# The o products of the attention by single heads, in two row halves of the array and two PSUM banks, and spread between second-layer products

## The chip, the cores and the metric

The kernel runs as one program on one core of a Trainium2 chip. The metric is the device time of one execution in microseconds. Before the change the median of three runs is 1733.42 us (1733.07 to 1734.48).

## What is computed

A linear attention over 8 batches, 8 heads, 576 positions and a head dimension of 64 feeds two mixing blocks of width 512 over the same positions:

```python
kv = np.einsum('bhsd,bhse->bhde', k, v)
out = np.einsum('bhsd,bhde->bhse', q, kv)
rms = np.sqrt(np.mean(out * out, axis=-1, keepdims=True) + 1e-06)
x = out / rms * g_norm                      # then (batch, 576, 512)
mixed = np.real(np.fft.fft(np.fft.fft(x, axis=1), axis=2))
u = x + mixed
ch = np.maximum(layer_norm(u) @ w_ch1, 0.0) @ w_ch2
x = u + ch
h = (x.transpose(0, 2, 1) @ U @ V).transpose(0, 2, 1)
u = x + h
return u + np.maximum(u @ w_ch1b, 0.0) @ w_ch2b
```

The change touches the second line alone, the product of q with the 64 by 64 matrix kv of each head, called the o products here.

## The kernel before

The weights of the first block are split into a high and a low part, and three products of the parts stand for one exact one. The positions of all batches together make nine blocks of 512. For each block a loop runs over `NF` = 16 slices of the hidden layer; step `n` emits on TensorE the first-layer products of slice `n` (`emit_l1`, lines 223 to 225, twelve of 128x512) and then the second-layer products of slice `n - 1` (`emit_l2`, lines 252 to 254, twelve of 128x512). All engines work in the order in which the kernel emits; nothing is reordered by a planner. The attention and the Fourier transform of batch `b` are cut into small tasks that hang on the steps of block `b - 1`: the list `side[n]` is run after the second-layer products of step `n`, and a single entry `fill[n]` is run between the first-layer products of step `n` and the second-layer products that follow them. `batch_tasks(b)` makes the lists `t[0]` to `t[13]` for the 16 steps. Batch 0 is computed before the loop starts, batch 1 beside block 0 (steps 0 to 15, in which weights are still being converted and the second-layer products are those of line 244), and batches 2 to 7 beside blocks 1 to 6.

`t_o(b, k)` makes one tile of the o products: up to 128 positions (98 in tile `k` = 4) by 512 columns. The matrices kv of two heads stand as two diagonal blocks of 64 by 64 in a 128 by 128 block of the buffer `kvbd`, whose other two blocks are zero. One product of TensorE takes 128 rows of q (two heads) as the stationary operand and 128 columns of `kvbd` as the moving one, and four products (line 397) fill the 512 columns of one PSUM bank. ScalarE then squares the bank (line 399), VectorE multiplies it by the norm's weight (line 401), sums the squares by head (line 404), scales (line 405), and GpSimd takes the power -1/2 (line 406). `t_norm` applies that a step later (lines 422 and 424). PSUM banks for such tasks come from `side_bank`: in the loop a ring of two banks (`ps_s`), before the loop six banks. Tiles 0 and 1 of a batch hang on step 0, tiles 2 and 3 on step 1, tile 4 on step 2; each pair runs back to back on TensorE.

Before the loop, `t_o(0, 0)` to `t_o(0, 4)` follow `t_kv_first`, and `keep_warm(54)` (line 413), 54 products of an identity, follows them on TensorE ahead of the first transform products (`seq_dft`, lines 495 to 501).

Of the kernel before, what the change touches and what calls it, by code (L numbers as in the profile page):

```python
# [13 lines left out]
AF = mybir.ActivationFunctionType  # L14
ALU = mybir.AluOpType
# [4 lines left out]
B, H, S, D = 8, 8, 576, 64  # L20
# [3 lines left out]
C = 128  # L24
# [7 lines left out]
NF = DFF // 128  # L32
# [13 lines left out]
def kernel(ctx: ExitStack, tc: tile.TileContext, qT, kvm, gn, w1a, w2a, w1b, w2b,  # L46
                      ucat, v4, tabs, outT):
    nc = tc.nc
# [14 lines left out]
    def whole(pool, shape, dt, name, tag=None, bufs=1):  # L63

        n = int(np.prod(shape[1:]))
        t = pool.tile([shape[0], -(-n // 16) * 16], dt, tag=tag or name, name=name, bufs=bufs)[:, 0:n]
        if len(shape) == 2:
            return t
        names = "abcd"[:len(shape) - 1]
        return t.rearrange(f"p ({' '.join(names)}) -> p {' '.join(names)}", **dict(zip(names, shape[1:])))  # L70
# [3 lines left out]
    def side_bank(nm):  # L74
        if early:
            k = len(early) % 6
            early.append(True)
            if k < 4:
                return ps_acc.tile([128, 512], F32, tag=f"acc{k}", name=nm)
        return ps_s.tile([128, 512], F32, tag="side", name=nm)  # L80
# [186 lines left out]
    gnb = at.tile([C, D], F32, name="gnb")  # L267
# [34 lines left out]
    kvbd = com.tile([128, 4, 128], F32, tag="kvbd", name="kvbd")  # L302
# [7 lines left out]
    def t_kv_mm(b, half):  # L310
        kv = st[b]["kv"]
        ps = kvps[b, half] = side_bank(f"kv{b}_{half}")
        for j in range(2):
            cols = slice(256 * half + 128 * j, 256 * half + 128 * j + 128)
            for t in range(KC):
                nc.tensor.matmul(out=ps[:, 128 * j:128 * j + 128], lhsT=kv[:, 0, t, cols], rhs=kv[:, 1, t, cols],
                                 start=(t == 0), stop=(t == KC - 1))
# [63 lines left out]
    def kv_back(b):  # L381
        for p in range(2):
            x = slice(64 * p, 64 * p + 64)
            nc.sync.dma_start(out=kvbd[x, :, x], in_=kv_d[b][p])
# [3 lines left out]
    def t_o(b, k):  # L388
        s = st[b]
        g, c, m = OT[k]  # L390
        if k == 0:
            s["x"] = at.tile([C, 2, 3, DM], F32, tag="xpn", name=f"x{b}")
            s["sq"] = at.tile([C, 5, DM], F32, tag="slot_b", name=f"sq{b}")
            s["ss"] = whole(at, [C, 5, H], F32, f"ss{b}", "ss", 2)
        ps = side_bank(f"o{b}_{k}")
        for j in range(4):
            nc.tensor.matmul(out=ps[:m, 128 * j:128 * j + 128], lhsT=s["q"][:, j, C * k:C * k + m],  # L397
                             rhs=kvbd[:, j, :], start=True, stop=True)
        nc.scalar.activation(out=s["sq"][:m, k, :], in_=ps[:m, :], func=AF.Square)
        heads = lambda v: v.rearrange("p (h d) -> p h d", d=D)  # L400
        nc.vector.tensor_tensor(out=heads(s["x"][:m, g, c]), in0=heads(ps[:m, :]),
                                in1=gnb[:m].unsqueeze(1).to_broadcast([m, H, D]), op=ALU.mult)
        ss = s["ss"][:m, k]
        nc.vector.reduce_sum(out=ss, in_=s["sq"][:m, k].rearrange("p (h d) -> p h d", d=D), axis=AX.X)
        nc.vector.tensor_scalar(out=ss, in0=ss, scalar1=1.0 / D, scalar2=EPS, op0=ALU.mult, op1=ALU.add)
        nc.gpsimd.tensor_tensor(out=ss, in0=ss, in1=nhalf[:m, :], op=ALU.pow)
# [8 lines left out]
    def t_norm(b, k):  # L415
        s = st[b]
        g, c, m = OT[k]
        xv = s["x"][:m, g, c].rearrange("p (h d) -> p h d", d=D)
        rs = s["ss"][:m, k]
        if b == 1 or b == 0 and k in (1, 2):  # L420
            for h in range(8):
                nc.scalar.activation(out=xv[:, h], in_=xv[:, h], func=AF.Copy, scale=rs[:, h:h + 1])
        else:
            nc.vector.tensor_tensor(out=xv, in0=xv, in1=rs.unsqueeze(2).to_broadcast([m, H, D]), op=ALU.mult)
        if c == 2:
            nc.scalar.activation(out=s["x"][0:RL + 1, 1, 2], in_=s["x"][64:64 + RL + 1, 0, 2], func=AF.Copy)

    def t_fold_s(b, c, p):
        s = st[b]
        if c == 0 and p == 0:  # L430
            s["f"] = at.tile([C, 2, 3, DM + 256], F32, tag="slot_a", name=f"f{b}")
            s["eh"] = at.tile([C, 2, 2, 2, 256], F32R, tag="slot_b", name=f"eh{b}")
            s["ez"] = at.tile([97, 2, 256], F32R, tag="ez", name=f"ez{b}")
            s["e288"] = e288[32:33]
        m = C if c < 2 else RL
        f, x = s["f"], s["x"]
        eng = nc.gpsimd if b and p else nc.vector
        eng.tensor_tensor(out=f[:m, p, c, 0:DM], in0=x[:m, 0, c], in1=x[:m, 1, c], op=(ALU.add, ALU.subtract)[p])

    def t_fold_e(b, c, p):  # L440
        m = C if c < 2 else RL
        f = st[b]["f"][:m, p, c]
        nc.vector.tensor_tensor(out=f[:, DM:DM + 256], in0=f[:, 1:257], in1=f[:, 511:255:-1],
                                op=(ALU.add, ALU.subtract)[p])
# [10 lines left out]
    def t_fold_h(b, c, p):  # L455
        s = st[b]
        f = s["f"][:, p, c]
        if c < 2:
            nc.scalar.activation(out=s["eh"][:, p, 0, c], in_=f[:, DM:DM + 256], func=AF.Copy)
        else:  # L460
            if p == 0:
                nc.scalar.activation(out=s["e288"], in_=f[32:33, DM:DM + 256], func=AF.Copy)
            pile(s["ez"][:, p], f[:, DM:DM + 256])
        if p == 0:
            m = C if c < 2 else RL
            nc.scalar.activation(out=xe0[:m, c, b:b + 1], in_=f[:m, 0:1], func=AF.Copy)

    def t_fold_l(b, c, p):
        s = st[b]
        f, eh = s["f"][:, p, c, DM:DM + 256], s["eh"]  # L470
        if c < 2:
            nc.vector.tensor_tensor(out=eh[:, p, 1, c], in0=f, in1=f32(eh[:, p, 0, c]), op=ALU.subtract)
        else:
            if p == 0:
                nc.vector.tensor_tensor(out=s["e288"], in0=f[32:33], in1=f32(s["e288"]), op=ALU.subtract)
            pile_low(s["ez"][:, p], f)
# [28 lines left out]
    def t_s1(b, p, ec):  # L505
        t_s1_mm(b, p, ec)
        t_s1_out(b, p, ec)
# [72 lines left out]
    def load_kv(b):  # L580
        kv = at.tile([128, 2, KC, DM], F32, tag="slot_a", name=f"kv{b}")
        for a in range(2):
            nc.sync.dma_start(out=kv[:, a], in_=kvm[b][:, a])
        st.setdefault(b, {})["kv"] = kv

    def batch_tasks(b):

        t = [[] for _ in range(14)]
        d, d1 = 0, SH if b == 1 else 0
        for c in range(3):  # L590
            ks = range(2 * c, min(2 * c + 2, 5))
            t[c + d][0:0] = [lambda k=k: t_o(b, k) for k in ks]
            t[c + d + 1] += [lambda k=k: t_norm(b, k) for k in ks]
            t[c + d + 3] += [lambda c=c, p=p: t_fold_s(b, c, p) for p in range(2)]
            t[c + d + 3].append(lambda c=c: t_fold_e(b, c, 0))
            t[c + d + 4] += [lambda c=c: t_fold_e(b, c, 1)]
            for p in range(2):
                t[c + d + 4 + p].insert(0, lambda c=c, p=p: t_fold_h(b, c, p))
                t[c + d + 4 + p].append(lambda c=c, p=p: t_fold_l(b, c, p))
            if c == 2 and 1 < b < B - 1 and b + 1 not in EARLY:  # L600
                fill[(b - 1) * NF + 11] = lambda: t_s2(b, 2)
            else:
                t[c + 9].append(lambda c=c: t_s2(b, c))
        for p in range(2):
            if d1:
                fill[8 + p] = lambda p=p: [t_s1(b, p, e) for e in range(2)]
            else:
                t[7 + p] += [lambda p=p, e=e: t_s1(b, p, e) for e in range(2)]
        if b + 1 < B:
            if b + 1 in EARLY:  # L610
                t[11].insert(0, lambda: kv_back(b + 1))
            else:
                t[7].append(lambda: load_kv(b + 1))
                for h in range(2):
                    t[11 + h].append(lambda h=h: t_kv_mm(b + 1, h))
                    t[12 + h].insert(0, lambda h=h: t_kv_out(b + 1, h))
            t[12].append(lambda: load_q(b + 1))
        return t
# [632 lines left out]
    fill = {}  # L1251
# [10 lines left out]
    with tc.manual_schedule():  # L1262
# [188 lines left out]
        def heads(n):  # L1451
            if n in mags:
                w_mags(*mags[n])
            if n + 2 < NP:
                split_w1(n + 2)

        for n in range(NP):
            i, j = n % NF, n // NF
# [143 lines left out]
```

## Time and profile before

| | |
|---|---|
| median of 3 runs | 1733.42 us |
| the profiled execution, its own time | 1734.35 us |
| its span, first to last instruction | 1732.6 us |
| granted TensorE clock, mean | 0.999 |

The page names the busy time of each engine: PE is the products on TensorE, PEld its weight loads, DVE is VectorE, ACT is ScalarE, POOL is GpSimd. A product of two 4-byte float operands (`f32` buffers) is executed as two records, one load and one product each: the 40 tiles have 160 products in line 397, and the trace has 320 records of each kind. A record's duration is longer than the step from one record to the next, because they overlap; the steps are read from the starts.

### The profile page before, as it was taken

How to read it: one execution, taken by the hardware profiler on the slowest of the kernel's cores; microseconds unless marked ns; L12 is line 12 of the kernel's file. 1: busy time of each engine (PE TensorE's matmuls, PEld its weight loads, DVE VectorE, ACT ScalarE, POOL GpSimd, SP SyncE). 2: the span in 40 equal slices, each digit the busy share in tenths (PEclk: the TensorE clock that was granted, in tenths of full speed). 3: DMA queues.
4: the chain of work that ended last, by engine and by line, in shares of the span. 5: the costliest groups of instructions: out<-in, count | busy, mean ns of one | idle time of the engine just before them, and what ended most of it. 6: DMA issues, size and time to landing. Idle time of an engine off the chain costs nothing.

```text
span 1732.6 us, 23201 instructions
## 1 busy us (share of the span) xinstructions
PE 1716.3 (99%) x8222; PEld 1426.1 (82%) x8222; DVE 1184.6 (68%) x1903; ACT 830.8 (48%) x1592; POOL 462.3 (27%) x362
## 2 busy tenths in 40 slices
PE   8999999999999999999999999999999999999999
PEld 8767788888888888888888888888888888888887
DVE  5899767778677686756676666448835963694285
ACT  5774344544435343343556565456445534552253
POOL 2346454455645446443322223000000000000000
PEclk9999999999999999999999999999999999999999
DMA  8666024150613416113368864767776776777676
GB/s 335 224 205 214 30 100 142 37 193 19 229 65 122 178 42 225 34 38 101 118 241 313 321 223 165 249 173 254 252 240 192 240 264 199 222 231 244 194 221 192
DMA packets 129011, 315.24 MB, mean 182 GB/s; under 512 B 20712, under 2 KB 20984, under 8 KB 127104
## 3 DMA queue, kind: packets, MB, share of 16 engines
q1 hardware_dynamic: 128896, 313.77, 54.4%
q8 instruction: 65, 1.06, 0.3%
q14 instruction: 50, 0.41, 0.1%
HBM read 238.83 MB, written 74.88 MB: 181 GB/s over the span
## 4 chain that ended last, share of the span: by engine, by line
PE 92%; DVE 0%; ACT 0%; issue 0%
PE y L1159 10%; PE yy L1239 10%; PE h L223 8%; PE h L224 8%; PE h L225 8%; PE acc L252 7%; PE acc L254 7%; PE acc L253 7%; PE z L1239 5%; PE zz L1159 5%; PE w L1239 3%; PE z L1159 3%; PE o L397 2%; PE pt L855 1%; PE u L880 1%; PE acc L257 1%
## 5 line engine op out<-in xcount | busy, mean ns | idle before, releaser
L199 POOL TENSOR_TENSOR w1l<-w,w1h 128x512 fp32r<-128x512 f32 x147 | 197.4, 1343 | 399.7 <-ACT w1h L198 384.2
L223 PE MATMUL h<-xl,w1h 128*128 128x512 f32 x576 | 231.1, 401 | 1.6 <-DVE xl L710 1.6
L225 PE MATMUL h<-xh,w1l 128*128 128x512 f32 x576 | 224.6, 390 | 0.5 <-POOL w1l L199 0.5
L224 PE MATMUL h<-xh,w1h 128*128 128x512 f32 x576 | 224.8, 390 | 0.0
L252 PE MATMUL acc<-w2h,gl 128*128 128x512 f32 x524 | 205.6, 392 | 0.0
L254 PE MATMUL acc<-w2h,gh 128*128 128x512 f32 x524 | 204.1, 390 | 0.0
L253 PE MATMUL acc<-w2l,gh 128*128 128x512 f32 x524 | 204.0, 389 | 0.0
L232 ACT ACTIVATE gh<-h 128x512 fp32r<-128x512 f32 x147 | 87.5, 595 | 227.3 <-PE h L225 224.9
L1159 PE MATMUL y<-xv,v 128*128 128x512 f32 x768 | 187.5, 390 | 2.7 <-ACT g L1096 2.7
L1096 ACT ACTIVATE g<-y 128x512 f32<-128x512 f32 x128 | 76.6, 598 | 204.1 <-PE y L1159 204.1
L1159 PEld LDWEIGHTS y<-xv,v 128*128 128x128 f32 x768 | 143.9, 188 | 34.1 <-ACT g L1096 4.4
L233 DVE SCALAR_TENSOR_TENSOR gl<-h,gh 128x512 fp32r<-128x512 f32 x147 | 100.8, 686 | 87.8 <-ACT gh L232 86.7
L209 DVE TENSOR_TENSOR w2l<-w,w2h 128x512 fp32r<-128x512 f32 x147 | 136.7, 930 | 34.1 <-ACT w2h L208 33.6
L223 PEld LDWEIGHTS h<-xl,w1h 128*128 128x128 f32 x576 | 108.3, 188 | 24.4 <-ACT w1h L198 2.1
L225 PEld LDWEIGHTS h<-xh,w1l 128*128 128x128 f32 x576 | 108.2, 188 | 24.3 <-POOL w1l L199 0.9
L224 PEld LDWEIGHTS h<-xh,w1h 128*128 128x128 f32 x576 | 108.4, 188 | 22.1 <-issue 1.9
L252 PEld LDWEIGHTS acc<-w2h,gl 128*128 128x128 f32 x524 | 98.4, 188 | 21.2 <-DVE gl L233 1.5
L254 PEld LDWEIGHTS acc<-w2h,gh 128*128 128x128 f32 x524 | 98.4, 188 | 20.6
L253 PEld LDWEIGHTS acc<-w2l,gh 128*128 128x128 f32 x524 | 98.4, 188 | 19.6
L208 ACT ACTIVATE w2h<-w 128x512 fp32r<-128x512 f32 x147 | 91.8, 625 | 40.8 <-PE acc L254 37.3
L198 ACT ACTIVATE w1h<-w 128x512 fp32r<-128x512 f32 x160 | 99.9, 624 | 12.3 <-DVE w L130 12.1
L1090 DVE TENSOR_TENSOR g<-zz,g 128x512 f32<-128x512 f32 x64 | 44.2, 691 | 89.7 <-ACT g L1096 77.4
(244 smaller groups left out, 3666.9 us busy)
## 6 DMA issues: line engine op xcount, KB each, us to landing
v<-wv_d SPq DMA_DIRECT2D x224, 512.0 KB, 3.7
wv_d<-vo SPq DMA_DIRECT2D x112, 256.0 KB, 3.0
kve<-in_kvm SPq DMA_DIRECT2D x40, 256.0 KB, 5.6
q<-in_qT SPq DMA_DIRECT2D x8, 1220.0 KB, 10.0
x_d<-res SPq DMA_DIRECT2D x36, 256.0 KB, 2.0
x2f<-x_d SPq DMA_DIRECT2D x36, 256.0 KB, 5.4
outT<-o SPq DMA_DIRECT2D x36, 256.0 KB, 2.7
u_d<-x SPq DMA_DIRECT2D x32, 256.0 KB, 2.1
```

Of the source, the lines that this page charges most:

```text
L198: nc.scalar.activation(out=ah, in_=a, func=AF.Copy)
L199: (nc.vector if n in on_dve else nc.gpsimd).tensor_tensor(out=al, in0=a, in1=f32(ah), op=ALU.subtract)
L209: nc.vector.tensor_tensor(out=cl, in0=c, in1=f32(ch), op=ALU.subtract)
L223: nc.tensor.matmul(out=h, lhsT=ah[:, kc, :], rhs=xl[:, kc, :], start=(kc == 0), stop=False)
L224: nc.tensor.matmul(out=h, lhsT=ah[:, kc, :], rhs=xh[:, kc, :], start=False, stop=False)
L225: nc.tensor.matmul(out=h, lhsT=al[:, kc, :], rhs=xh[:, kc, :], start=False, stop=(kc == 3))
L233: nc.vector.scalar_tensor_tensor(out=gl, in0=h, scalar=0.0, in1=f32(gh), op0=ALU.max, op1=ALU.subtract)
L252: nc.tensor.matmul(out=a, lhsT=gl[:, tt], rhs=ch, start=s, stop=False)
L253: nc.tensor.matmul(out=a, lhsT=gh[:, tt], rhs=cl, start=False, stop=False)
L254: nc.tensor.matmul(out=a, lhsT=gh[:, tt], rhs=ch, start=False, stop=e)
L1159: nc.tensor.matmul(out=dst, lhsT=w[:, c], rhs=r[:, k], start=p in (0, 1, 3) and k + n == 0, stop=k == 1 and n == 2, skip_group_check=True)
L1239: nc.tensor.matmul(out=dst[mp], lhsT=w[:, c], rhs=r, start=p in (0, 1, 6, 3) and i + n == 0, stop=i == 7 and n == 2, skip_group_check=True)
```

## The change

`t_o` takes two banks for a tile. Each product now takes 64 rows of q and the 64 by 64 block of one head; the even heads use partitions 0 to 63 and write the first 256 columns of one bank, the odd heads use partitions 64 to 127 and write the other bank. So a tile has eight products of 64 rows, 128 stationary columns and 64 moving columns in place of four of 128, 128 and 128. ScalarE and VectorE read each bank for itself, with 256 columns each. For batches 2 to 7 the odd tiles go to `fill`, ahead of the second-layer products of steps 1 and 2, and the even tiles stay in `side`, so that no two tiles follow each other on TensorE without products of a layer between them. Batch 1 and batch 0 keep their order.

```diff
-        ps = side_bank(f"o{b}_{k}")
+        ps = [side_bank(f"o{b}_{k}_{p}") for p in range(2)]
         for j in range(4):
-            nc.tensor.matmul(out=ps[:m, 128 * j:128 * j + 128], lhsT=s["q"][:, j, C * k:C * k + m],
-                             rhs=kvbd[:, j, :], start=True, stop=True)
-        nc.scalar.activation(out=s["sq"][:m, k, :], in_=ps[:m, :], func=AF.Square)
-        heads = lambda v: v.rearrange("p (h d) -> p h d", d=D)
-        nc.vector.tensor_tensor(out=heads(s["x"][:m, g, c]), in0=heads(ps[:m, :]),
-                                in1=gnb[:m].unsqueeze(1).to_broadcast([m, H, D]), op=ALU.mult)
+            for p in range(2):
+                e = slice(64 * p, 64 * p + 64)
+                nc.tensor.matmul(out=ps[p][:m, 64 * j:64 * j + 64], lhsT=s["q"][e, j, C * k:C * k + m],
+                                 rhs=kvbd[e, j, e], start=True, stop=True)
+        heads = lambda v, p: v.rearrange("p (h e d) -> p h e d", e=2, d=D)[:, :, p]
+        for p in range(2):
+            pv = ps[p][:m, 0:256].rearrange("p (h d) -> p h d", d=D)
+            nc.scalar.activation(out=heads(s["sq"][:m, k, :], p), in_=pv, func=AF.Square)
+            nc.vector.tensor_tensor(out=heads(s["x"][:m, g, c], p), in0=pv,
+                                    in1=gnb[:m].unsqueeze(1).to_broadcast([m, H // 2, D]), op=ALU.mult)
...
-            t[c + d][0:0] = [lambda k=k: t_o(b, k) for k in ks]
+            if b == 1:
+                t[c + d][0:0] = [lambda k=k: t_o(b, k) for k in ks]
+            else:
+                for k in ks:
+                    n = (k + 1) // 2
+                    if k % 2:
+                        fill[(b - 1) * NF + n] = lambda k=k: t_o(b, k)
+                    else:
+                        t[n].insert(0, lambda k=k: t_o(b, k))
```

## Rows read from the trace of the kernel before

**Rows 1.** The page: busy time by engine, and the chain that ended last.
```profile
PE 1716.3 (99%) x8222; PEld 1426.1 (82%) x8222; DVE 1184.6 (68%) x1903; ACT 830.8 (48%) x1592; POOL 462.3 (27%) x362
...
PE 92%; DVE 0%; ACT 0%; issue 0%
```

**Rows 2.** TensorE in order of time, batch 7: start, length, operation, count.
```profile
713.75 0.39 PE L254 MATMUL acc<-w2h,gh 128*128 128x512 f32 x1
713.98 1.95 PE L397 MATMUL o<-kvbd,q 128*128 128x128 f32 x16
715.68 0.48 PE L223 MATMUL h<-xl,w1h 128*128 128x512 f32 x1
716.00 0.40 PE L224 MATMUL h<-xh,w1h 128*128 128x512 f32 x1
...
721.23 1.04 PE L397 MATMUL o<-kvbd,q 128*98 128x128 f32 x8
722.02 0.48 PE L223 MATMUL h<-xl,w1h 128*128 128x512 f32 x1
```

**Rows 3.** Weight loads by line and shape: busy us, mean ns, idle before.
```profile
L397 PEld LDWEIGHTS o<-kvbd,q 128*128 128x128 f32 x256 | 32.3, 200 | 4.4 <-DVE kvbd L338 2.1 <-ACT kvr L377 0.9 <-issue 0.5
...
L397 PEld LDWEIGHTS o<-kvbd,q 128*98 128x98 f32 x64 | 7.8, 164 | 1.1 <-issue 0.5
...
L541 PEld LDWEIGHTS s<-tab,y 128*34 128x34 f32 x32 | 3.5, 109 | 0.5
...
L696 PEld LDWEIGHTS ftr<-ident,un 128*128 128x128 f32 x12 | 1.3, 140 | 0.6 <-issue 0.5
...
L696 PEld LDWEIGHTS ftr<-ident,un_z 33*128 33x128 f32 x4 | 0.3, 138 | 0.1
```

**Rows 4.** Weight loads in order of time: two after a pause, four of 33 rows.
```profile
50.01 0.32 PEld L696 LDWEIGHTS ftr<-ident,un_z 33*128 33x128 f32 x4
...
55.56 0.19 PEld L223 LDWEIGHTS h<-xl,w1h 128*128 128x128 f32 x1 [1.78 <-ACT w1h L198]
55.67 0.19 PEld L224 LDWEIGHTS h<-xh,w1h 128*128 128x128 f32 x1
```

**Rows 5.** TensorE in order of time around 34-column products.
```profile
668.88 0.39 PE L225 MATMUL h<-xh,w1l 128*128 128x512 f32 x1
669.11 0.28 PE L541 MATMUL s<-tab,y 128*34 128x258 f32 x1
...
670.53 0.40 PE L252 MATMUL acc<-w2h,gl 128*128 128x512 f32 x1
```

**Rows 6.** ScalarE and VectorE from PSUM, by line and shape, blocks 1 to 6.
```profile
L399 ACT ACTIVATE sq<-o 128x512 f32<-128x512 f32 x24 | 14.3, 595 | 17.7 <-PE o L397 17.6
...
L545 ACT ACTIVATE de<-s 128x258 f32<-128x258 f32 x12 | 4.6, 387 | 35.3 <-PE s L543 35.3
...
L401 DVE TENSOR_TENSOR x<-o,gnb 128x512 f32<-128x512 f32 x24 | 16.4, 685 | 9.9 <-ACT sq L399 9.9
...
L546 DVE TENSOR_TENSOR de<-s,de 128x258 f32<-128x258 f32 x12 | 5.0, 419 | 22.8 <-ACT de L545 22.8
```

**Rows 7.** Batch 1 in order of time, TensorE and ScalarE.
```profile
65.73 2.05 PE L397 MATMUL o<-kvbd,q 128*128 128x128 f32 x16 [0.70 <-ACT kvr L377]
...
75.52 0.48 PE L223 MATMUL h<-xl,w1h 128*128 128x512 f32 x1
...
77.05 1.06 ACT L399 ACTIVATE sq<-o 128x512 f32<-128x512 f32 x2
```

**Rows 8.** Batch 0 in order of time.
```profile
20.39 12.22 PE L413 MATMUL warm<-ident 128*128 128x128 f32 x108
32.37 0.38 PE L495 MATMUL s<-tab,eh 128*128 128x290 f32 x1
```

**Rows 9.** Batch 4, first tile, in order of time: TensorE and VectorE.
```profile
387.39 1.95 PE L397 MATMUL o<-kvbd,q 128*128 128x128 f32 x16
...
390.02 0.68 DVE L401 TENSOR_TENSOR x<-o,gnb 128x512 f32<-128x512 f32 x1
```

## Prediction, made before the changed kernel was run

> **What bounds the kernel now.** First the page's busy times and its chain that ended last: TensorE is busy 99% of the span and 92% of the chain is its products; VectorE (68%), ScalarE (48%) and GpSimd (27%) follow it [rows 1]. So work on those three costs nothing while TensorE's next instruction isn't kept waiting, and a nanosecond on TensorE is a nanosecond of the span. Then TensorE in order of time around one pair of tiles and one single tile [rows 2]: the reader should take starts, not lengths. Between 512-column products a start follows a start in 0.23 us (713.75 to 713.98). The 16 records of two tiles run from 713.98 to 715.68, and the next step, 0.32, is 0.09 longer than the usual 0.23. So a pair costs 1.70 + 0.09 = 1.79, a tile 0.893 us and a record 112 ns; the 98-row tile costs 0.79 + 0.09 = 0.88, 109 ns a record. The 30 tiles of batches 2 to 7 are 6 x (4 x 0.893 + 0.88) = 26.7 us, all 40 about 36: that is all that the change can work on.
>
> **What a record of an o product waits for.** A record is a weight load and a product, and a load runs beside the product before it. Two things could set the 112 ns: the load of 128 columns, or the streaming of 128 moving columns. The loads by shape [rows 3] last 200 ns at 128 columns, 164 at 98 and 109 at 34, about 0.9 ns a column over a constant latency; in order of time a load that starts after a pause at 55.56 is followed by the next at 55.67, so 128 columns occupy the load path some 107 ns [rows 4]. Streaming takes about the same: with 98 stationary columns the load shrinks, yet the record still takes 109. Both are at the limit. Rows don't count: of the transposing loads, the one of 33 rows lasts 138 ns and the one of 128 rows 140 [rows 3], and the four of 33 rows follow each other every (0.32 - 0.14) / 3 = 0.06 us although they stream 33 columns only [rows 4]. That is the row that speaks most against the change: it halves the moving columns (streaming 53 ns) and the rows, but each head keeps a load of 128 columns, and there are twice as many, 16 loads of 107 ns a tile in place of 8. Nothing can be won unless two loads are under way at once; if they are, perfectly, the two halves bring the tile back to 0.89.
>
> **The change part by part.**
>
> TensorE, batches 2 to 7. The trace has no two loads into different rows, so the price of a tile lies between both halves overlapped, 8 x 112 = 0.89, and one load after the other, 16 x 112 = 1.79; for the 98-row tile, whose load is about 82 ns, between 8 x 87 = 0.70 and 16 x 87 = 1.39. I take a value between. A float product is two records, so the order is load and product of the even head twice, then of the odd head twice. In the trace a load never starts ahead of the start of the product before it. If that order holds and loads of different halves may overlap, the odd head's first load starts when the even head's second product is taken up, at 107 + 53 = 160 ns, its second at 267, and the next even head's first at 320: 2 x (107 + 53) + about 10 = 330 ns for the four records of two heads. A tile is 4 x 0.33 = 1.32, 0.43 more than now; the 98-row tile 4 x (2 x (82 + 53) + 10) = 1.12, 0.24 more. A batch: 4 x 0.43 + 0.24 = 1.96; six: **+11.8 us**.
>
> Entering and leaving the half-row form: no row shows it in a running stream. Nearest is the 34-column product [rows 5]: it starts 0.23 after the product before, twelve of them take 1.42 or 0.118 each, and the next follows at once. I take 0.3 us for 40 tiles. The Trainium skill, TensorEngine Tiling (Array Packing), Key Properties, says that changing the tiling mode drains the engine; these rows show no drain for narrow columns, and no row shows row halves.
>
> Eviction. ScalarE takes 595 ns for 512 columns and 387 for 258, VectorE 685 and 419 [rows 6]: two halves cost 0.18 and 0.15 us more a tile, some 7 and 6 us over 40 tiles on engines with idle time, while VectorE may read the first bank as ScalarE reads the second (0.39 + 2 x 0.42 = 1.23 against 0.60 + 0.69 = 1.29). Cover: TensorE. It ends where TensorE wants the bank back.
>
> The alternation is needed for just that, since a tile now takes the whole ring of two banks. Between two tiles lie twelve products of a layer, 12 x 0.227 = 2.72 us. The latest eviction is that of the first tile of a batch: its products end near 387.39 + 0.89 + 0.16 = 388.44, the multiply starts at 390.02 behind the adds of the block before and takes 0.68 [rows 9], so it ends 2.3 us after, 2.4 with the split. The next tile starts at 387.39 + 0.893 + 0.09 + 2.72 = 391.09, so it fits by 0.2; I charge nothing, and 0.3 x 6 = 2 us if it does not fit. Behind a late multiply on VectorE queue the reduction, the scaling, and then the low part of the hidden values that second-layer products need (line 233); the odd tiles reach GpSimd's power earlier relative to `t_norm` than the pair does now. No DMA moves.
>
> Batch 1 keeps pairs, so its second tile waits for the first one's banks: end of the last record (0.27 after its start, less the usual step 0.11) + 0.39 + 0.42 + 0.05 = 1.0 us after the first pair. With 1.32 a tile the first pair ends at 65.73 + 1.32 + 1.0 + 1.32 = 69.4, where it ended at 65.73 + 1.79 = 67.52: +1.85. The second pair starts 1.70 ahead of 75.52 [rows 7], now at 75.67, its first tile ends 76.99; ScalarE squares it at 77.2 at the earliest (it came at 77.05 before, busy with weights), the bank is free at 78.05, and the pair ends at 79.4, not 75.52: +3.85. The fifth tile adds 0.24: **+4.1**. Queued behind this on TensorE are the layers of block 0; later waits of theirs may give some back, which I don't count.
>
> Batch 0. `keep_warm` follows the o products and the first transform product starts at its last step, 32.37 [rows 8]: TensorE has no gap there, so the five tiles' 1.96 us pass on: **+2.0**, with 0.4 as the least (VectorE's extra 0.75, partly in its gaps).
>
> Sum: 11.8 + 0.3 + 4.1 + 2.0 = +18.2. The profiled execution is 1734.35 us (span 1732.6 and 1.75 around it), 0.93 above the median of the runs: 1734.35 + 18.2 - 0.93 = **1751.6 us**.
>
> **The rivals.**
>
> Both halves fully overlapped. For: nothing in the rows forbids a load into other rows to start early. Batches 2 to 7: 0 for the large tiles, 6 x -0.18 for the small; batch 1 still waits for banks (end of second pair 78.8, +3.3, less 0.18); batch 0 +0.4; entering 0.3. Sum +2.8, or +1 if block 0 gives some back: 1733.4 + 2.8 = 1736.2. The Trainium skill, the same section, says that different tiles can run loads and products in parallel; by that sentence this would be the case.
>
> One load at a time: the halves do not run together and the change doesn't do what it says. For: in every row loads follow each other. A batch 4 x 0.893 + 0.52 = 4.1: six are 24.6, batch 1 +6.2 (pairs end at 70.3 and 81.2, then 0.5), batch 0 +4.1, entering 0.3: +35.2, 1768.6.
>
> A drain at each change of form, on top of the forecast: what the overlap hides now would show. Entering, 0.39 - 0.23 = 0.16; leaving, 1.04 - 0.79 = 0.25 [rows 2]; 40 x 0.41 = 16.4: 1768. Against it: [rows 5]. The skill's sentence on the drain is this rival.
>
> The other side, faster: a load of 64 rows occupies half the time, and the halves overlap. Then a tile is 8 x 58 = 0.46, 0.43 less: batches 2 to 7 -12.8, batch 1 +2.4 (the second pair still waits for ScalarE at 77.05), entering 0.3: -10.1, 1723.3. It decides from the point where a record of a half takes under 50 ns. Against it: 33 rows load no faster than 128 [rows 3]. For it: those loads are of another form.
>
> **How the numbers follow.** Forecast 0.30, full overlap 0.22, one load at a time 0.24, drain 0.08, faster 0.16. A measurement of this kernel can tell about 0.2%, 3.5 us, from no change. Faster: 0.16 and 0.01 of full overlap, 0.17. Same: most of full overlap, 0.19. Slower: 0.64. The range goes from the middle of the fast case, 1723, to 1772, over the serial one with its unknowns (the 2 us of banks, 1 to 2 of batch 0); about 0.08 lies below and 0.06 above.
>
> **What would show it.** Steps between starts in line 397's records, in blocks 1 to 6: four in 0.33 us (forecast), 0.22 (overlap), 0.45 (serial), under 0.2 (faster). The distance from the last layer product before a tile to the first after it tells the drain. In batch 1 a wait on VectorE's line 401 in front of tiles 1 and 3; in batches 2 to 7 none: such waits would make the alternation the failed step. Wrong altogether would be a kernel that changes by more than 36 us, since only the o products and banks are touched.

## Result, and the profile after

The changed kernel takes 1752.77 us (median; 1750.88 to 1754.32) and the kernel before, run beside it, 1733.95: a ratio of 1.0105 with a 95% interval of 1.0093 to 1.0117, or 18.8 us more. The forecast was 1751.6 and slower. The sum came out nearly right, but by luck: two of its terms were wrong in opposite directions. The profiled execution of after took 1754.32 us, its span is 1752.4.

The page after, busy time by engine and the chain that ended last, answers to [rows 1]:

```profile
PE 1734.5 (99%) x8542; PEld 1431.6 (82%) x8542; DVE 1192.0 (68%) x1943; ACT 833.3 (48%) x1632; POOL 464.5 (27%) x362
...
PE 97%; DMA 1%; DVE 1%; ACT 1%; SPq 0%; issue 0%; POOL 0%; DVEq 0%; ACTq 0%
```

TensorE is the bound as it was. It has 18.2 us more busy time and 320 records more; every other engine gained under 8 us.

TensorE in order of time around one tile of after (start, length, operation, count), to be held against [rows 2]:

```profile
294.81 0.39 PE L225 MATMUL h<-xh,w1l 128*128 128x512 f32 x1
295.13 1.11 PE L399 MATMUL o<-kvbd,q 64*128 64x64 f32 x16
296.17 0.50 PE L223 MATMUL h<-xl,w1h 128*128 128x512 f32 x1
296.51 0.39 PE L224 MATMUL h<-xh,w1h 128*128 128x512 f32 x1
```

The weight loads of the same tile, in three windows: the first 70 ns, the first 170 ns, and the whole.

```profile
295.13 0.19 PEld L399 LDWEIGHTS o<-kvbd,q 64*128 64x128 f32 x2 [0.35 <-issue]
...
295.13 0.30 PEld L399 LDWEIGHTS o<-kvbd,q 64*128 64x128 f32 x4 [0.35 <-issue]
...
295.13 0.97 PEld L399 LDWEIGHTS o<-kvbd,q 64*128 64x128 f32 x16 [0.35 <-issue]
296.17 0.19 PEld L223 LDWEIGHTS h<-xl,w1h 128*128 128x128 f32 x1
```

Two things are to be seen here. First, the halves run together. The first load lasts 0.183 us, and two of them fit into 0.190: they start 7 ns apart. (A record doesn't name its half; that two such loads are of different halves follows from the halves in turn, below, where loads of one half go 0.11 apart.) The next two end 0.11 later. So each pair of loads takes the 0.11 us that one full load took, and 16 records of half the rows cost what 8 full ones did: (0.97 - 0.19) / 7 = 0.11 us a pair. Four records take 0.22, not the 0.33 of the forecast. Second, the way in and out is no longer free. From the layer product to the first record it is 295.13 - 294.81 = 0.32 where it was 0.23, the first load of the tile starts with its product and not beside the one before it, and at the end the load of line 223 starts 0.07 after the last o load has ended, where loads of layer products run ahead.

The cost of a tile follows from four starts: from the layer product ahead of it to the second one behind it, less the two steps of 0.227 that these would take alone. After: 296.51 - 294.81 - 0.454 = 1.25 us. Before: (716.00 - 713.75 - 0.454) / 2 = 0.90 from [rows 2]. So a tile costs 0.35 more, and all 24 large tiles of batches 2 to 7 show it within 0.01; the 98-row tile costs 0.15 more.

Loads and evictions by line and shape (busy us, mean ns | idle before), which answer to [rows 3] and [rows 6]:

```profile
L399 PEld LDWEIGHTS o<-kvbd,q 64*128 64x128 f32 x512 | 35.7, 207 | 14.8 <-issue 6.3 <-DVE ss L408 2.1 <-DVE x L428 2.1
...
L404 ACT ACTIVATE sq<-o 128x256 f32<-128x256 f32 x64 | 21.3, 384 | 30.1 <-PE o L399 30.0
...
L405 DVE TENSOR_TENSOR x<-o,gnb 128x256 f32<-128x256 f32 x64 | 24.1, 416 | 22.2 <-ACT sq L404 22.2
```

The load of 64 rows isn't shorter than the one of 128 rows (0.20 us in [rows 3]). The half evictions took 384 and 416 ns, as estimated.

The start of the kernel shows a third thing that the prediction hadn't looked at, the granted clock. Here are two stretches of each kernel (busy us and instructions of the engines, then the granted clock, DMA share, GB/s). Before:

```profile
15.20:25.40 10.20, 10.20 (x79) 10.20 (x78) 8.34 (x17) 8.06 (x22) 7.51 (x5) 0.83 1.03 408
...
69.80:76.60 6.80, 6.80 (x33) 4.59 (x32) 6.17 (x13) 4.82 (x10) 2.83 (x3) 1.00 0.32 95
```

After:

```profile
15.20:25.40 10.20, 10.20 (x85) 10.08 (x84) 8.33 (x22) 7.47 (x23) 7.28 (x5) 0.50 1.03 409
...
69.80:76.60 6.80, 6.28 (x34) 5.45 (x33) 4.00 (x11) 3.72 (x9) 3.48 (x3) 0.50 0.38 139
```

In after TensorE has half its clock (1.2 of 2.4 GHz) over the o products of batch 0 and the warming products behind them, 10.2 us long, where before had it for a third of that (3.4 us). It has half its clock once more in batch 1, for 6.8 us, where before had the full clock. The length of the first stretch isn't fixed: with the same products in batch 0, the profiled execution of the halves in turn has 10.2 us and that of the pairs kept 6.8 (both below); of the seven with batch 0 as before, six have 3.4 and one has none.

### The profile page after: what moved, and what is told of

The parts are those of the page before. It is cut to its first block, busy times and chain, and to the rows that moved or that the text cites. A ratio compares the mean times of both kernels' runs of the same rounds, so it can differ in the third digit from the quotient of the medians.

```text
span 1752.4 us, 23925 instructions
## 1 busy us (share of the span) xinstructions
PE 1734.5 (99%) x8542; PEld 1431.6 (82%) x8542; DVE 1192.0 (68%) x1943; ACT 833.3 (48%) x1632; POOL 464.5 (27%) x362
## 4 chain that ended last, share of the span: by engine, by line
PE 97%; DMA 1%; DVE 1%; ACT 1%; SPq 0%; issue 0%; POOL 0%; DVEq 0%; ACTq 0%
PE y L1171 10%; PE yy L1251 10%; PE h L223 8%; PE h L224 8%; PE h L225 8%; PE acc L252 7%; PE acc L254 7%; PE acc L253 7%; PE z L1251 5%; PE zz L1171 5%; PE acc L244 3%; PE o L399 3%; PE w L1251 2%; PE z L1171 2%; PE pt L867 1%; PE u L892 1%
## 5 line engine op out<-in xcount | busy, mean ns | idle before, releaser
L198 ACT ACTIVATE w1h<-w 128x512 fp32r<-128x512 f32 x160 | 99.8, 624 | 11.9 <-DVE w L130 11.8
```

The costliest lines, as they stand in the source:

```text
L198: nc.scalar.activation(out=ah, in_=a, func=AF.Copy)
```

## Experiments

**Full rows, 64 columns.** As after, but each product takes all 128 rows of q, so that no two can share the array.

```diff
-                nc.tensor.matmul(out=ps[p][:m, 64 * j:64 * j + 64], lhsT=s["q"][e, j, C * k:C * k + m],
-                                 rhs=kvbd[e, j, e], start=True, stop=True)
+                nc.tensor.matmul(out=ps[p][:m, 64 * j:64 * j + 64], lhsT=s["q"][:, j, C * k:C * k + m],
+                                 rhs=kvbd[:, j, e], start=True, stop=True)
```

> As the changed kernel (two banks, alternation, eight products of 64 moving columns a tile), but each product uses all 128 rows of q, so no form of the array changes and no two loads go to different rows. Theory (the load of 128 columns sets the step, and the changed kernel won back the doubled number of loads only by running the halves side by side): a record every 112 ns, 16 records 1.79 us a tile against the changed kernel's 1.24 from product to product, so +0.55 a large tile and +0.35 to +0.7 a small one, 15 to 17 us over batches 2 to 7; batch 0 and 1 add some 2 to 5: 1768 to 1774 us. If in batch 0 the clock still stays at half for 10 us, half rows are not what held it down; with 3.4 us it would be them. Rival (64 moving columns stream in 53 ns and that is the limit): about 60 ns a record, 0.96 a tile and no cost of changing form, 1742 us or less.

Measured: 1776.52 us, against 1734.75 for before in the same comparison, ratio 1.0243 (1.0228 to 1.0258). TensorE around one tile, and the 98-row tile of the same batch:

```profile
308.68 0.39 PE L225 MATMUL h<-xh,w1l 128*128 128x512 f32 x1
308.91 1.89 PE L399 MATMUL o<-kvbd,q 128*128 128x64 f32 x16
310.61 0.48 PE L223 MATMUL h<-xl,w1h 128*128 128x512 f32 x1
310.92 0.40 PE L224 MATMUL h<-xh,w1h 128*128 128x512 f32 x1
...
326.99 1.52 PE L399 MATMUL o<-kvbd,q 128*98 128x64 f32 x16
328.32 0.48 PE L223 MATMUL h<-xl,w1h 128*128 128x512 f32 x1
```

The 16 records take 310.61 - 308.91 = 1.70, some 0.11 each although they stream 64 columns in place of 128: the load of 128 columns alone sets the step of a record. In the 98-row tile, with 98 columns to load and the same 64 to stream, they take 328.32 - 326.99 = 1.33, or 0.083 each: the step goes with the columns that are loaded. The way in is 0.23 again and the way out 0.31, as in before. So the overlap of after is real and comes from the row halves, and so does the price of the way in and out. The time is a little over what was expected; the granted clock was between 0.50 and 0.54 in each 4 us from 16 to 32, longer than in after. That speaks against the thought that it is the half rows which hold the clock down.

**Halves in turn.** As after, but all even heads of a tile before all odd ones.

```diff
-        for j in range(4):
-            for p in range(2):
+        for p in range(2):
+            for j in range(4):
```

> As the changed kernel, but each tile makes its four products of the even heads first and then the four of the odd heads, so neighbours in the order are mostly of one half. Theory (the halves overlap only because they stand next to each other in the order; loads are taken in order): 112 ns a record, a tile 1.79 + 0.35 = 2.14 against 1.24, +0.9 a large tile and +0.5 to +0.9 a small one, 25 to 27 us over batches 2 to 7, and 4 to 8 in batches 0 and 1: 1782 to 1788 us. Rival (a load into other rows is pulled ahead over any distance): the same 0.056 us a record, 1752.8 us.

Measured: 1769.32 us, ratio 1.0199 (1.0184 to 1.0214), between the two expectations, so both were wrong. The loads of one tile, from its start on up to the time when the first odd load comes in (300.93), then TensorE:

```profile
300.43 0.63 PEld L399 LDWEIGHTS o<-kvbd,q 64*128 64x128 f32 x5 [0.35 <-issue]
```

```profile
300.11 0.39 PE L225 MATMUL h<-xh,w1l 128*128 128x512 f32 x1
300.43 1.60 PE L399 MATMUL o<-kvbd,q 64*128 64x64 f32 x16
301.96 0.50 PE L223 MATMUL h<-xl,w1h 128*128 128x512 f32 x1
302.30 0.39 PE L224 MATMUL h<-xh,w1h 128*128 128x512 f32 x1
```

Five even loads go alone, 0.11 apart, in 0.5 us. Then a load starts only 0.06 behind the one before it, and from there on two rows of loads run, each 0.11 apart. By this spacing it is the first odd load, while three even ones are still to come; its product starts with it, and the products of those three at 301.04, 301.15 and 301.26. So loads and their products are pulled ahead of records of the other half, past about three of them, but not any distance. The tile costs 302.30 - 300.11 - 0.454 = 1.74, which is 0.49 more than with alternating heads, and the 98-row tile 0.39 more; 24 x 0.49 + 6 x 0.39 = 14.1 us of the 16.5 between the two kernels.

**The order alone.** The products and the single bank of before, with the changed order of the tiles (tiles 1 and 3 of batches 2 to 7 in `fill`).

> The kernel before with the changed order of the tiles alone (odd tiles of batches 2 to 7 ahead of second-layer products), and its own products in one bank. Theory (the order costs nothing by itself; all of the change's cost in batches 2 to 7 comes from its products): 1734.0 us, within 2. Rival (odd tiles ahead of the second layer delay VectorE's low part of the hidden values, 0.18 us a batch in the changed kernel's trace, and more at other places): 1735 to 1737 us.

Measured: 1734.21 us, ratio 0.9997 (0.9988 to 1.0007). One odd tile, now between a first-layer and a second-layer product:

```profile
295.41 0.39 PE L225 MATMUL h<-xh,w1l 128*128 128x512 f32 x1
295.64 1.05 PE L397 MATMUL o<-kvbd,q 128*128 128x128 f32 x8
296.45 0.48 PE L252 MATMUL acc<-w2h,gl 128*128 128x512 f32 x1
296.76 0.40 PE L253 MATMUL acc<-w2l,gh 128*128 128x512 f32 x1
```

A tile alone costs 296.76 - 295.41 - 0.454 = 0.90, as one of a pair does. Moving the tiles costs nothing, so the whole loss lies in the form of the products and in their banks.

**The pairs kept.** The products and two banks of after, in the order of before: tiles 0 and 1, and 2 and 3, back to back in every batch.

> The changed kernel's products and banks with the order of before, so pairs of tiles follow each other in all batches. Theory (the ring of two banks makes the second tile wait for the first one's eviction): about 1 us for the second pair of a batch and 2.2 for the first pair, whose eviction stands behind the adds of the block before, less 0.35 for one change of form saved a pair: 6 x (1.85 + 0.65) = 15 us, 1765 to 1770 us, more if the clock falls in these pauses. Rival (the alternation buys nothing): 1752.8 us or, by the changes of form saved, 12 x 0.35 = 4 less, 1748.6 us.

Measured: 1795.89 us, ratio 1.0349 (1.0334 to 1.0365), far above every expectation. What TensorE waited for by the o products of line 399 (us, times, longest):

```profile
PE o L399 <- DVE x L405: 18.6, 14, 2.0
```

The first pair of a batch in order of time, and the second tile of its second pair:

```profile
298.43 1.11 PE L399 MATMUL o<-kvbd,q 64*128 64x64 f32 x16
301.43 1.43 PE L399 MATMUL o<-kvbd,q 64*128 64x64 f32 x16 [1.90 <-DVE x L405]
302.80 0.79 PE L223 MATMUL h<-xl,w1h 128*128 128x512 f32 x1
303.39 0.63 PE L224 MATMUL h<-xh,w1h 128*128 128x512 f32 x1
...
312.08 1.74 PE L399 MATMUL o<-kvbd,q 64*128 64x64 f32 x16 [0.93 <-DVE x L405]
```

And the windows around the first pair:

```profile
298.00:302.60 4.60, 2.70 (x35) 2.17 (x33) 3.31 (x7) 1.69 (x4) 1.28 (x2) 1.00 0.29 113
302.60:306.00 3.40, 3.40 (x12) 2.66 (x11) 2.11 (x5) 1.18 (x3) 2.88 (x2) 0.53 0.03 7
```

In each of batches 2 to 7 the second tile of the first pair waits 1.9 us for VectorE to give the banks back, and that of the second pair 0.9, which the expectations had priced. They had named but not priced what came behind it: here for 3.4 us the granted clock is about half, and a layer product lasts 0.63 us in place of 0.39. Each of these twelve waits is followed by such a stretch, of 3.4 or 6.8 us. Over the kernel the mean clock is 0.981 against 0.995 in after: 0.019 x 1793.5 - 0.005 x 1752.4 = 25 us of lost TensorE time, and the waits for banks are 18.6 against 1.4, 17 more. Together that is 42 us of the 43 between this kernel and after. So the alternation isn't decoration: with it, no tile of batches 2 to 7 waits for a bank.

**Batch 0 as before.** As after, but batch 0 uses one bank and four full products a tile (`if b == 0:` with the old body).

> The changed kernel with batch 0 as before (one bank, four products of 128 rows a tile). Theory (batch 0 costs through the clock: its halves kept TensorE at half speed for 10.2 us and not 3.4, and the steps of the warm products show 2.9 us lost there, of which 2.6 are left at 59 us): 1752.8 - 2.6 = 1750.2 us, and the clock is back after 3.4 us. Rival (the clock's length is chance, and batch 0 costs nothing by itself): 1752.8 us with a long half-speed stretch still.

**Batches 0 and 1 as before.** The same with `if b < 2:`.

> The changed kernel with batches 0 and 1 as before, so only batches 2 to 7 use the halves. Theory (of the 18.8 us, batches 2 to 7 cost 6 x (4 x 0.35 + 0.16) = 9.4 and 1 more in waits for the low part of the hidden values; the rest is batch 0 and the bank waits and the clock in batch 1): 1734.7 + 10.4 = 1745 us. Rival (my sum: batches 2 to 7 cost 12): 1746.8 us; a third: block 0 gives batch 1's loss back at its later waits, then 1750.

Measured, in one comparison with before at 1734.12: 1749.63 us (ratio 1.0092, 1.0077 to 1.0107) with batch 0 as before, 1746.17 us (1.0067, 1.0051 to 1.0084) with both. So batches 2 to 7 cost 1746.17 - 1734.12 = 12.0 us, batch 1 some 3.5, batch 0 some 3.1 to 3.3 (from the medians, or from the differences to the before of each comparison). With batch 0 as before the clock at the start recovers early again:

```profile
15.20:18.70 3.50, 3.50 (x19) 3.50 (x18) 2.63 (x5) 1.29 (x3) 1.21 (x1) 0.51 1.00 417
18.70:25.40 6.70, 6.70 (x62) 6.70 (x61) 5.71 (x13) 6.70 (x20) 6.27 (x5) 1.00 1.04 404
```

That is about the whole of batch 0: 10.2 us at half clock in place of 3.4 is (10.2 - 3.4) / 2 = 3.4 us of TensorE. Batch 1 on TensorE, first with row halves (batch 0 as before), where line 409 has the o products:

```profile
68.23 1.43 PE L409 MATMUL o<-kvbd,q 64*128 64x64 f32 x16 [0.73 <-DVE x L415]
...
69.99 0.63 PE L224 MATMUL h<-xh,w1h 128*128 128x512 f32 x1
...
79.58 1.43 PE L409 MATMUL o<-kvbd,q 64*128 64x64 f32 x16 [0.93 <-DVE x L415]
80.94 0.50 PE L223 MATMUL h<-xl,w1h 128*128 128x512 f32 x1
```

Then with batch 1 as before:

```profile
74.38 1.95 PE L398 MATMUL o<-kvbd,q 128*128 128x128 f32 x16
76.08 0.48 PE L223 MATMUL h<-xl,w1h 128*128 128x512 f32 x1
```

Each pair waits for its bank (0.73 and 0.93 us), 3.4 us go at half clock behind the first wait, and the second pair ends 80.94 - 76.08 = 4.9 us later. Part of that is given back: set product against product, the trace with batch 0 as before lags the one with both by 5.1 us at 110 us and by 3.2 from 140 us on. With both as before TensorE waits 0.36 us at 119.53 for GpSimd's line 199 and 0.88 at 136.65 for VectorE's line 542; behind the late batch 1 it waits for neither. One caution: the profiled execution with batch 0 as before has another 3.4 us at half clock from 56.2 to 59.6, ahead of batch 1's o products, which neither kernel beside it has. The order alone and the next kernel (one product of half the rows) have one there too, so it comes and goes without the change, and it isn't in the 3.5: that next kernel is 1.6 us behind before at 58 us and 0.1 at 67, since before waits there for transfers.

**One product of half the rows in a tile of full ones.** The kernel before, where in batches 2 to 7 the second of the four products of a tile is cut into two of 64 columns: the first takes 64 rows, the second 128.

```diff
+            if b < 2 or j != 1:
...
+            for p in range(2):
+                e, r = slice(64 * p, 64 * p + 64), slice(0, 64) if p == 0 else slice(0, 128)
+                nc.tensor.matmul(out=ps[:m, 128 * j + 64 * p:128 * j + 64 * p + 64],
+                                 lhsT=s["q"][r, j, C * k:C * k + m], rhs=kvbd[r, j, e], start=True, stop=True)
```

> The kernel before (one bank, pairs), but in batches 2 to 7 the second of a tile's four products is cut in two of 64 moving columns, the first of these with 64 rows alone, the second with 128 rows. So each of 30 tiles has two records more and one change of form in and out, with no two halves to run together. To be read against the next kernel, which has the same products without the change of form. Theory (changing the form of the array costs about 0.35 us in and out, as seen around the changed kernel's tiles): 30 x 0.35 = 10 us more than that one, 1751 us. Rival (the 0.35 us is the filling of two halves, not a drain): the same as that one, 1741 us.

**The same with full rows.** Both products take 128 rows (`r = slice(0, 128)`), all else is the same.

> The kernel before, but in batches 2 to 7 the second of a tile's four products is cut in two of 64 moving columns, both with all 128 rows. Theory (a record costs its load, 108 to 112 ns, whatever it streams): two records more, 30 x 0.22 = 6.6 us, 1741 us. Rival (64 columns cost half): two records of 112 become four of 56, no change, 1734.7 us.

Measured, beside before at 1734.12: 1751.61 us with one product of 64 rows (ratio 1.0101, 1.0086 to 1.0116), 1741.11 us with full rows (1.0042, 1.0027 to 1.0057). The two kernels differ in nothing but the rows of one product a tile, with the same number of loads, columns and banks; that product makes TensorE go into the other form and out of it once. It costs 10.5 us for 30 tiles, 0.35 us each; tile against tile in the two traces it is 0.33. TensorE over a pair of tiles, with one product of 64 rows (line 403 is the cut product):

```profile
288.16 0.38 PE L398 MATMUL o<-kvbd,q 128*128 128x128 f32 x2
288.47 0.80 PE L403 MATMUL o<-kvbd,q 64*128 64x64 f32 x4
289.11 0.89 PE L398 MATMUL o<-kvbd,q 128*128 128x128 f32 x6
```

And with full rows:

```profile
285.16 0.38 PE L398 MATMUL o<-kvbd,q 128*128 128x128 f32 x2
285.38 0.56 PE L403 MATMUL o<-kvbd,q 128*128 128x64 f32 x4
285.77 0.89 PE L398 MATMUL o<-kvbd,q 128*128 128x128 f32 x6
```

The way in takes 0.31 in place of 0.22, and the four records with the way out 0.64 in place of 0.39: 0.09 and 0.25, together 0.34. These are the sizes that a tile of after shows. The Trainium skill, TensorEngine Tiling (Array Packing), Key Properties, says that a change of the tiling mode drains the engine; it gives no time for it. The two kernels agree with it so far as they show the price, 0.34 us for in and out; what TensorE does in that time they don't show.

**Batch 1 spread too.** Batch 0 as before, and the tiles of batch 1 alternate with layer products like the others (the exception for `b == 1` is taken out).

> As the kernel with batch 0 old (1749.6 us), and batch 1's odd tiles too go ahead of second-layer products, so that no batch has pairs of tiles in halves. Theory (batch 1 costs 3.3 us because each pair's second tile waits for the banks, and the clock falls in that pause): the waits and the fall go, the five tiles' changes of form stay at 5 x 0.33 = 1.7, some of it given back at the later waits of block 0: 1746 to 1748 us. Rival (ScalarE and VectorE, which convert weights beside block 0, set batch 1's loss, wherever its tiles stand): 1749.6 us or more.

Measured: 1748.95 us beside before at 1734.82, ratio 1.0078 (1.0061 to 1.0094), where pairs in batch 1 gave 1.0092 (1.0077 to 1.0107) in another comparison. The intervals overlap, so nothing is shown to be gained. The trace says why the theory's 2 to 3 us didn't come. TensorE, the second and third tile of batch 1:

```profile
70.13 1.11 PE L409 MATMUL o<-kvbd,q 64*128 64x64 f32 x16
...
76.65 1.43 PE L409 MATMUL o<-kvbd,q 64*128 64x64 f32 x16 [1.78 <-DVE x L415]
```

ScalarE's square of the second tile, in all engines' order of time:

```profile
75.24 0.63 ACT L198 ACTIVATE w1h<-w 128x512 fp32r<-128x512 f32 x1
75.76 0.65 ACT L414 ACTIVATE sq<-o 128x256 f32<-128x256 f32 x2
```

The second tile's products are done by 71.2, but ScalarE, busy with the weights of block 0 (line 198 and the lines of the conversion ahead of it), squares them at 75.76 only. The wait for a bank is gone from the pairs and stands, twice as long, in front of the third tile, and 3.4 us at half clock follow it too, from 79.0 to 82.4. One tile now owns both banks, so any late eviction stops the next one.

## Why the prediction was right, and where it was not

**The bound and the record's limit: right.** TensorE stayed the bound [rows 1]. That the load of 128 columns sets the step is shown by the full-row products of 64 columns, 0.11 us each, and that the rows don't matter by the five even loads of the halves in turn, of 64 rows and 0.11 apart too. The faster rival (a load of 64 rows in half the time) fell on that: loads of 64 rows last as long as those of 128.

**The overlap of the halves, +11.8: wrong.** The step that failed was "a load never starts ahead of the start of the product before it", which holds in the trace of before, where, as it says, no two loads go into different rows, but not across the halves: their loads start 7 ns apart. The rival of full overlap had this right. The Trainium skill, TensorEngine Tiling (Array Packing), Key Properties, says that different tiles can run loads and products in parallel; the trace agrees, with these 7 ns. This term should have been 0 for the large tiles. That the rows of before couldn't decide it was said; the value that was taken between the ends rested on an order of loads that no row showed across halves.

**The change of form, +0.3: wrong.** It costs 0.35 us for each large tile of batches 2 to 7 and 0.15 for each small one, net of some 0.2 that the overlap gives a small tile back: 24 x 0.35 + 6 x 0.15 = 9.3 us. The rival had taken 0.41 from the steps at the edges of before's tiles: 0.16 in and 0.25 out; measured were 0.09 and 0.25. It had been given 0.08 because the 34-column products of [rows 5] enter and leave without a gap. Those use all 128 rows, though, and the row that was missing was one with half of them.

**Batches 2 to 7 together: 12.1 predicted, 12.0 measured, by an error on each side.** So the agreement is luck. The parts measured are 9.3 for the form and, at the second-layer products, some 0.2 a batch for `gl`, 1.2 in all. The loads of line 252 waited for VectorE's line 233 like this before (us, times, longest):

```profile
PEld acc L252 <- DVE gl L233: 1.5, 7, 0.2
```

and after:

```profile
PEld acc L252 <- DVE gl L233: 3.8, 7, 1.3
```

The prediction had named that queue on VectorE and charged nothing for it. Product against product, the profiled execution with batches 0 and 1 as before lags before by 0.5 us ahead of batch 2, by 11.0 more behind batch 7 and by 0.3 more from 997 us on: 11.8, the difference of the two spans. So of the 12.0 about 1 us lies outside batches 2 to 7, and 0.5 inside them is assigned to nothing. The 1.3 in the last line is a single wait at 1005 us, far behind the change (0.86 on TensorE). The kernel with the cut product of full rows has a longer one (0.95 on TensorE), and the one with batches 0 and 1 as before, from which the 12.0 comes, a short one (the 0.3 at 997 us), so it isn't the row halves' own.

**The alternation fits: right.** No product of batches 2 to 7 waited for a bank, and the order alone cost nothing. What it is worth was far underrated, 0.3 x 6 = 2 us: keeping the pairs cost 43, 17 of it in the waits and 25 in the stretches at half clock that followed each of them.

**Batch 1, +4.1: size near, reason partly wrong.** The waits for banks were 0.5 to 0.9 us, near the 1.0 predicted. ScalarE did not hold up the second pair as [rows 7] had suggested, while the half clock, which wasn't counted, did. The 4.9 us lost by then shrank to 3.5, a give-back that the prediction mentioned and left out. In the profiled execution of after, with 6.8 us at half clock there, batch 1 costs 5.2.

**Batch 0, +2.0: too low, and for another reason.** The tiles follow each other there, so the form changes once, and the halves overlap: little should have been lost. The o products start at 14.25 before and at 14.35 after; they end where the warming products start, at 20.39 before [rows 8] and at 21.95 after, and half of the loss comes only behind that, with the warming products at half clock. It is the longer stretch at half clock, 3.4 us by its length, 3.1 to 3.3 by the runs. Why the chip granted half the clock for two to three times as long isn't settled; the full-row variant, with the same many short products, had it for longer still.

**The sum.** 18.2 predicted, 18.8 measured: 12.0 + 3.5 + 3.1 to 3.3. The profiled execution of after splits otherwise: set product against product it lags before by 2.6 us ahead of batch 1, 5.2 more ahead of batch 2, 10.9 more behind batch 7 and 1.1 more at 1005 us, 19.8 in all, the difference of the two spans. So what falls to batch 0 and what to batch 1 hangs on the stretches at half clock. The likeliest case wasn't the one that happened. It was two rivals at once, full overlap (+2.8) and a change of form at each tile (+16.4), which add up to 19.2 (near the 18.8 partly by chance too, since neither has the clock in it); the prediction had hung the change of form on its own forecast only and so never wrote that sum down.

## What to carry to other kernels

Half the rows and half the columns don't pay where the load of the stationary operand sets the step: two loads at once give back just what twice as many loads take, and every stretch in the other form costs a way in and out, so a stretch of one tile loses; the long one of batch 0 gained nothing either. When an unknown lies between two mechanisms, price each and their combinations; a value between them stands on neither. And a tile that takes the whole ring of banks needs other work behind it on TensorE, for the wait is not the worst of it.

## What the runs showed of the hardware

- Weight loads into different row halves start 7 ns apart and take 0.11 us a pair at 128 columns, the same as one load of 128 rows; loads and their products are pulled ahead past about three records of the other half, not past eight.
- Going from full to half rows and back cost 0.09 us in and 0.25 us out, with a single product as with sixteen records.
- Where the pairs were kept, each of the twelve waits on TensorE in batches 2 to 7 (1.9 us in the first pair of a batch, 0.9 in the second) was followed by 3.4 or 6.8 us at half clock; the 0.9 us wait in batch 1 of the same kernel was not. In batches 2 to 7 of after, where no such wait stands, the clock stayed at 1.00.
